# Exponentiating 5 of 16 key tiles per full unit as int16 bit patterns on VectorE, with shifts on Pool and sums and masks on TensorE

## The chip, the cores and the metric

The kernel runs on one core of a Trainium2 chip. The metric is device time in microseconds (us), the median of several executions. The kernel before takes 1201.22 us (three runs, 1200.22 to 1213.29). A difference of 2% counts. All runs below are on one core. Each experiment was timed in three rounds against the kernel before on the same chip; the experiments ran on several chips, on which the kernel before took 1202 to 1206 us (medians).

## The reference

Two attention blocks on inputs of 2048 x 512, each with 32 heads of width 16. Their outputs are laid side by side.

```python
def _A_ref(x, wqkv, wo):                       # "full": every key
    q, k, v = split(x @ wqkv)                  # 32 heads of 16
    scores = einsum("bhqd,bhkd->bhqk", q, k) * (Dh ** -0.5)
    o = einsum("bhqk,bhkd->bhqd", softmax(scores), v)
    return merge(o) @ wo
# _B_ref ("window"): the same with
    mask = (idx[:, None] - idx[None, :] >= 0) & (idx[:, None] - idx[None, :] < 256)
    scores = where(mask, scores, -1e9)
# ... setup, reshapes and the final concatenate cut
```

## The kernel before

The work comes in units of 4 heads by 512 queries: 32 full units of 16 key tiles and 32 window units. A tile is one head's 128 keys by 512 queries. Three tiles make a slot, and a slot has one tile of scores, three banks wide and with two buffers, in PSUM, the memory that TensorE's products go to. TensorE writes the scores, ScalarE exponentiates the slot in one instruction, and TensorE multiplies by the values (with a column of ones for the row sum). Projections are woven between slots in steps, and VectorE copies their results out of PSUM. A guard is a small product of this kind that gives each query an offset for its scores.

```python
def scores(self, slot):
    sps = self.ps.tile([P, SLOT, 512], FP32, name="sps", tag="sps", bufs=2)
    for b, jb in enumerate(slot["jobs"]):
        ...
        if b == 0:                       # whole-array product, overwritten by the next one
            self.nc.tensor.matmul(sps[:, 0, 0:WARM], lhsT=kT[:, gg, k0:k0 + P],
                                  rhs=qT[:, gg, 0:WARM], start=True, stop=True)
        for kt, q0, q1, o in jb.subs:
            self.nc.tensor.matmul(sps[:, b, o:o + q1 - q0], ..., tile_position=(32 * jb.j, 0))

def exps(self, slot):
    ...
    nc.scalar.activation(out=pT[:, b:e, :n], in_=sps[:, b:e, :n], func=ACT.Exp, scale=SCALE)
    # window blocks: VectorE multiplies by a triangle, or Pool selects (cut)

# run(), one slot after another:
    self.exps(sl)
    self.scores(slots[s + 2])
    self.values(...)                     # products with the values of earlier slots
    # then normalisation work that is due, then woven projection steps
```

The whole-array product has no use for the result. It keeps the array busy; b1_no_warm below shows what that does for the clock.

## Time and profile before

| engine | busy us | share of the 1204.9 us |
|---|---|---|
| ScalarE | 1094.0 | 91% |
| TensorE | 957.8 | 79% |
| VectorE | 309.1 | 26% |
| Pool | 141.4 | 12% |

The mean granted TensorE clock, as a share of full speed, was 0.958. A busy share is an average over the whole span. The pace is better read from the distance between the starts of neighbouring exponentials: 1.330 us per slot, 811 slots.

### The profile page before, as it was taken

The page shows a single profiled execution, that of the slowest core. Times are in us where ns is not written, and L with a number is a line of the kernel's source. Part 1 is how long each engine was busy: PE and PEld are TensorE (multiplying, and loading weights), DVE is VectorE, ACT ScalarE, POOL GpSimd, SP SyncE. Part 2 cuts the span into 40 slices and gives each one's busy share as a digit, 9 for nine tenths or more (in the row PEclk, how much of TensorE's full clock was granted, in tenths as well). Part 3 has the DMA queues.
Part 4 walks back from the last instruction along what each step waited for, and adds up shares of the span by engine and source line. Part 5 has one row for each costly group of instructions (what it writes and reads, how often), then busy time and mean ns, then how long its engine had stood idle before and what let it go on. Part 6 is the DMA issues. An engine that isn't in the chain of part 4 may idle for free.

```text
span 1204.9 us, 18272 instructions
## 1 busy us (share of the span) xinstructions
PE 957.8 (79%) x6762; PEld 281.9 (23%) x6859; DVE 309.1 (26%) x698; ACT 1094.0 (91%) x840; POOL 141.4 (12%) x349
## 2 busy tenths in 40 slices
PE   4888888888788888888888888868885888878754
PEld 1222222222222222222222222212221222222211
DVE  1232121133222233322233232322232222321102
ACT  2799999999899999999999999969995999999960
POOL 4000000011000011210121111111111110211100
PEclk8999999999999999899999999989997999998995
DMA  6011320111121101111111111211111111111011
GB/s 143 19 32 24 76 49 20 37 24 35 35 57 33 35 20 29 37 44 32 43 33 40 31 35 42 31 43 32 25 32 29 36 40 33 29 27 30 15 26 42
DMA packets 72921, 44.48 MB, mean 37 GB/s; under 512 B 45440, under 2 KB 64128, under 8 KB 72832
## 3 DMA queue, kind: packets, MB, share of 16 engines
q1 hardware_dynamic: 71248, 41.73, 16.0%
q10 hardware_dynamic: 1584, 1.57, 0.5%
q8 instruction: 54, 0.88, 0.3%
q14 instruction: 35, 0.29, 0.1%
HBM read 4.19 MB, written 4.19 MB: 7 GB/s over the span
## 4 chain that ended last, share of the span: by engine, by line
ACT 45%; PE 10%; issue 8%; SPq 3%; DMA 2%; DVE 2%; ACTq 0%; DVEq 0%
ACT pT L339 45%; PE sps L316 3%; PE sps L321 3%; PE ms L156 2%; PE op L371 2%; SPq L408 1%; SPq L268 1%; DMA out_dram<-ob 1%; DVE ob L300 1%; DMA oTa<-on 1%; DMA rb<-rrow 1%; DVE osb L385 1%; SPq L188 0%; DMA rrow<-den 0%; DVE pT L350 0%
## 5 line engine op out<-in xcount | busy, mean ns | idle before, releaser
L339 ACT ACTIVATE pT<-sps 128x1536 bf16<-128x1536 f32 (+4 forms) x827 | 1086.1, 1578 | 44.5 <-PE sps L321 34.3
L316 PE MATMUL sps<-qTa,kTa 128*128 128x512 bf16 x683 | 261.3, 383 | 131.1 <-ACT pT L339 125.8
L371 PE MATMUL op<-pT,va 128*32 128x512 bf16 x2048 | 275.8, 394 | 1.6 <-ACT pT L339 0.5
L321 PE MATMUL sps<-qTa,kTa 32*128 32x512 bf16 x2048 | 276.9, 389 | 0.0
L352 POOL TENSOR_SCALAR_AFFINE_SELECT pT<-pT 128x256 bf16<-128x256 bf16 (+2 forms) x224 | 105.2, 488 | 908.8 <-issue 532.4
L321 PEld LDWEIGHTS <-kTa 32*128 32x128 bf16 x2048 | 68.0, 91 | 347.5 <-issue 347.5
L371 PEld LDWEIGHTS <-va 128*32 128x32 bf16 x2048 | 69.0, 93 | 156.8 <-issue 155.8
L316 PEld LDWEIGHTS <-kTa 128*128 128x128 bf16 x683 | 65.8, 96 | 146.8 <-issue 124.4
L350 DVE TENSOR_TENSOR pT<-pT,mlo 128x128 bf16<-128x128 bf16 (+2 forms) x256 | 77.0, 345 | 85.7 <-ACT pT L339 84.7
L316 PE MATMUL sps<-qTb,kTb 128*128 128x512 bf16 x128 | 50.8, 396 | 32.7 <-ACT pT L339 30.8
L385 DVE COPY osb<-op 128x512 f32<-128x512 f32 x64 | 44.2, 691 | 87.4 <-PE op L371 87.2
L401 DVE TENSOR_TENSOR on<-osb,rb 128x512 bf16<-128x512 f32 x64 | 46.4, 726 | 77.3 <-DMA rb<-rrow 44.7
L300 DVE CAST ob<-ms 128x512 bf16<-128x512 f32 x32 | 22.1, 689 | 153.0 <-PE ms L156 153.0
L321 PE MATMUL sps<-qTb,kTb 32*128 32x384 bf16 (+2 forms) x704 | 58.0, 286 | 0.0
L371 PE MATMUL op<-pT,vb 128*32 128x384 bf16 (+2 forms) x704 | 49.6, 295 | 9.9 <-DVE osb L385 5.7
L262 DVE CAST qs<-ms 128x512 bf16<-128x512 f32 x31 | 21.3, 688 | 121.4 <-PE ms L156 121.4
L156 PE MATMUL ms<-wo,oTa 128*128 128x512 bf16 x51 | 19.9, 466 | 31.9 <-DMA oTa<-on 28.7
L392 DVE RECIPROCAL den<-den 128x16 f32<-128x16 f32 x64 | 15.1, 241 | 76.0 <-DMA den<-osb 76.0
L321 PEld LDWEIGHTS <-kTb 32*128 32x128 bf16 x704 | 17.0, 93 | 74.8 <-issue 74.8
L156 PE MATMUL ms<-xT,wq 128*128 128x512 bf16 x96 | 31.4, 384 | 3.7 <-issue 2.9
L156 PE MATMUL ms<-xT,wk 128*128 128x512 bf16 x94 | 30.3, 388 | 4.6 <-issue 1.7
L244 DVE CAST vb<-ms 128x512 bf16<-128x512 f32 x16 | 11.1, 691 | 83.1 <-PE ms L156 83.1
(47 smaller groups left out, 280.6 us busy)
## 6 DMA issues: line engine op xcount, KB each, us to landing
rb<-rrow SPq DMA_DIRECT2D x64, 256.0 KB
out_dram<-ob SPq DMA_DIRECT2D x32, 128.0 KB
kTa<-ksta SPq DMA_DIRECT2D x32, 64.0 KB
qTa<-qs SPq DMA_DIRECT2D x128, 16.0 KB
oTa<-on SPq DMA_DIRECT2D x128, 16.0 KB
kTb<-kstb SPq DMA_DIRECT2D x128, 16.0 KB
qTb<-qs SPq DMA_DIRECT2D x128, 16.0 KB
oTb<-on SPq DMA_DIRECT2D x128, 16.0 KB
```

The lines of the kernel that those rows point to most:

```text
L156: self.nc.tensor.matmul(bank, lhsT=lhs(c), rhs=rhs(c), start=(c == 0), stop=(c == NC - 1))
L262: copy(out=qs[:], in_=bank)
L300: self.nc.vector.tensor_copy(out=ob[:], in_=bank)
L316: self.nc.tensor.matmul(sps[:, 0, 0:WARM], lhsT=kT[:, gg, k0:k0 + P], rhs=qT[:, gg, 0:WARM], start=True, stop=True)
L321: self.nc.tensor.matmul(sps[:, b, o:o + q1 - q0], lhsT=kT[r, gg, k0:k0 + P], rhs=qT[r, gg, q0:q1], start=True, stop=True, tile_position=(3 ...
L339: nc.scalar.activation(out=pT[:, b:e, :n], in_=sps[:, b:e, :n], func=ACT.Exp, scale=SCALE)
L350: nc.vector.tensor_mul(out=v, in0=v, in1=self.mlo[:, 0:e - b, :])
L352: nc.gpsimd.affine_select(v, v, pattern=[[0, e - b], [-1, P]], compare_op=ALU.is_ge, fill=0.0, base=-1, channel_multiplier=1)
L371: self.nc.tensor.matmul(u["t"][32 * jb.j:32 * jb.j + 32, q0:q1], lhsT=self.v[jb.inst, kt][:, h * VP:h * VP + 32], rhs=slot["pT"][:, b, o:o ...
L385: nc.vector.tensor_copy(out=osb[:], in_=op[:])
L392: nc.vector.reciprocal(out=den[:], in_=den[:])
L401: nc.vector.tensor_mul(out=on[:], in0=osb[:], in1=st["rb"][:])
```

## The change

The intent is to take load from ScalarE, the bound. In each full unit 5 of the 16 key tiles (3 in the first unit) are exponentiated on VectorE: scale the score, round it to int16, read the bits as bf16. Two shifted copies made on Pool, weighted by two scaled copies of the values and summed on TensorE, smooth that rough exponential. A bias on ScalarE's exponentials and a lift in the scores keep both kinds on one scale. The masks of the window units move to TensorE, as products of an identity with a mask, and the whole-array product goes.

```diff
-QRING = (3, 4)
-KRING_B = 10
-VRING_B = 12
-LAGS = (6, 11, 22)
+QRING = (3, 2)
+KRING_B = 6
+VRING_B = 9
+LAGS = (7, 12, 23)
+D_KTS = (1, 4, 7, 10, 13)
 ...
     def scores(self, slot):
         sps = self.ps.tile([P, SLOT, 512], FP32, name="sps", tag="sps", bufs=2)
+                nc.tensor.matmul(sps[:, b, o:o + n * P], lhsT=self.ident[:],
+                                 rhs=self.mask[:, k:k + n, :], start=first, stop=False,
+                                 skip_group_check=True)
 ...
-            if b == 0:
-                self.nc.tensor.matmul(sps[:, 0, 0:WARM], lhsT=kT[:, gg, k0:k0 + P],
-                                      rhs=qT[:, gg, 0:WARM], start=True, stop=True)
 ...
             nc.scalar.activation(out=pT[:, b:e, :n], in_=sps[:, b:e, :n], func=ACT.Exp,
-                                 scale=SCALE)
+                                 scale=SCALE, bias=self.bias[:])
 ...
+            nc.vector.tensor_scalar(out=y[:, jb.j, :].bitcast(I16), in0=sps[:, b, :],
+                                    scalar1=0.0, scalar2=BITS, op0=ALU.max, op1=ALU.mult)
+            grp["n"] += 1
+            if grp["n"] == GH:
+                for c in SHIFTS:
+                    z = self.tile([P, GH, 512], BF16, "z", 4)
+                    nc.gpsimd.tensor_scalar(out=z[:].bitcast(I16), in0=y[:].bitcast(I16),
+                                            scalar1=c, scalar2=1.0, op0=ALU.add, op1=ALU.mult)
 ...
-            nc.vector.tensor_mul(out=on[:], in0=osb[:], in1=st["rb"][:])
+            nc.gpsimd.tensor_mul(out=on[:], in0=osb[:], in1=st["rb"][:])
 ...  (slot building, rings, plan of the woven steps cut)
```

## The prediction

> **What bounds the kernel now.** I began with the page's engine totals and slices, then the chain that ended last, then the groups kept apart by shape, then the chain and the timeline of short stretches.
>
> ```profile
> PE 957.8 (79%) x6762; PEld 281.9 (23%) x6859; DVE 309.1 (26%) x698; ACT 1094.0 (91%) x840; POOL 141.4 (12%) x349
> ACT  2799999999899999999999999969995999999960
> ACT 45%; PE 10%; issue 8%; SPq 3%; DMA 2%; DVE 2%; ACTq 0%; DVEq 0%
> ```
>
> ScalarE is full from the third slice to the last but one, and everything else has room. The chain gives it only 45% because a chain of overlapped instructions is cut in many pieces. The groups and a piece of the chain give the pace:
>
> ```profile
> L339 ACT ACTIVATE pT<-sps 128x1536 bf16<-128x1536 f32 x782 | 1055.9, 1619 | 40.9 <-PE sps L321 32.0 <-issue 5.5 <-POOL pT L352 1.4
> L339 ACT ACTIVATE pT<-sps 128x1024 bf16<-128x1024 f32 x9 | 9.9, 1105 | 1.2 <-POOL pT L352 0.8 <-issue 0.4
> ...
> 602.27 1.28 ACT pT L339
> 603.60 1.25 ACT pT L339
> 604.95 1.25 ACT pT L339
> 606.27 1.26 ACT pT L339
> 607.61 1.27 ACT pT L339
> ```
>
> One record of 1536 elements lasts 1619 ns, but neighbours start 1.33 us apart (of 775 pairs in the trace the tenth percentile and the median are 1329 and 1330 ns). Where a 1024-element exponential is followed closely, starts are 903 ns apart. So the pace is 0.833 ns per element plus about 50 ns. There are 2432 tiles of work (32 full units of 64, 32 window units of 12), three to a slot, so 811 slots: 811 x 1.330 = 1079 us. The trace has the first exponential at 34.3 us and the last end at 1164.9: 1131 us, of which some 52 are stalls. Then 40 us of tail. Sum 1205.
>
> TensorE in one slot, from the timeline:
>
> ```profile
> 700.79 0.38 PE L316 MATMUL sps<-qTa,kTa 128*128 128x512 bf16 x1 [0.32 <-ACT pT L339]
> 701.10 0.39 PE L321 MATMUL sps<-qTa,kTa 32*128 32x512 bf16 x3
> 701.42 0.40 PE L371 MATMUL op<-pT,va 128*32 128x512 bf16 x3
> 701.97 0.38 PE L156 MATMUL ms<-xT,wq 128*128 128x512 bf16 x1 [0.16 <-issue]
> 702.39 0.69 DVE L262 CAST qs<-ms 128x512 bf16<-128x512 f32 x1 [7.83 <-PE ms L156]
> ```
>
> The whole-array matmul of L316, whose result the next one overwrites, holds the array 0.31 us; three row-tiled scores 0.32; three column-tiled values some 0.32. A change of tiling costs about 0.1 us over the 0.215 us at which equal matmuls follow one another. The slot needs about 0.95 us of the 1.33, with 0.53 us more where a projection step is woven in.
>
> **What the Trainium skill says.**
> - "ScalarE: Activation LUTs", What ACT_TABLE_LOAD costs: an ACTIVATE with immediate scale and bias takes 186 ns + 0.833 ns per element, and each [128,1] pointer operand adds about 93 ns. The slope agrees (1445 ns shortest at 1536, 1018 at 1024: 0.834); the fixed part here is 165 ns, nearer to the form without a pointer. The change gives every exponential a bias tile. No run so far shows what that costs from start to start.
> - "GPSIMD Engine Reference", 4.1 Engine selection: one-input elementwise work is roughly at line rate, two-input work about twice slower than VectorE. The one-input selects here take 287, 401 and 514 ns at best for 128, 256 and 384 elements: 0.89 ns per element over 174.
> - "SBUF — State Buffer", Who interferes with whom: GpSimd and a VectorE instruction in a two-port mode, or with two SBUF inputs, exclude each other; other VectorE work does not. The new exponentials read PSUM, so they should not be touched. No run here shows it.
>
> **The change, part by part.**
> ScalarE: 31 units give up 5 x 4 tiles and the first 3 x 4: 632. Each is the third of a slot, so 632 slots have two tiles for ScalarE and the other 1800 - 1264 = 536 fill 179 slots of three. 632 x 0.903 + 179 x 1.330 = 809 us, 270 less than before. The bias pointer could add 811 x 0.093 = 75; I take two thirds, 50.
>
> VectorE: 632 tiles of 128x512 from PSUM at 0.69 us (its casts and copies of that shape are 691 ns) = 436 us. Masks (77) and the final scaling (46) leave it: 309 - 123 + 436 = 622 us. Not a bound by its sum.
>
> Pool: 158 groups of four tiles, two shifts each, 316 instructions of 2048 elements. Estimate from the selects: 174 + 2048 x 0.89 = 2.0 us, so 632 us; 64 scalings with two inputs, estimate 1.3 us each, 82; memsets 36; the selects (105) go. About 750 us. In a full unit the five groups ask for 20 us, plus 2 of other work, while the 20 slots with two tiles and 1.3 of three take ScalarE 20 to 22: Pool keeps up with little to spare, and the window slots give it rest.
>
> TensorE: L316 goes, 811 x 0.31 = 251 us. Vector groups need three value products for one: 158 x 3 sets of four column tiles at 0.215 = 102 us, in place of 632/3 x 0.32 = 67. ScalarE's values are gathered over two slots, four columns at once, so fewer changes of tiling. Masks in the scores: 640 identity products, 1024 columns per three tiles, 0.43 us and one change of tiling in each of 128 window slots = 69. The sum falls to about 750 us, under a slot's 0.9. In window slots masks, six partial scores and values come near 1.5 us against 1.33: 128 x 0.15 = 19 us lost.
>
> What I think takes much of the gain back is VectorE's **order**. Program order there is exponential of slot s, then a cast of a projection step woven into s, then the exponential of s+1. Call E the end of ScalarE's slot s. The cast's matmuls come after the scores of s+2, which wait for E: 0.05 + 0.32 + 0.1 + 0.215 + 0.416 (701.97 to 702.39 above) puts the cast at E + 1.1; 0.72 and 0.69 later the exponential of s+1 is done, at E + 2.5; only then can the scores of s+3 be written, and ScalarE starts s+3 at about E + 2.97. With two score buffers it would have started at E + 1.81. So 1.16 us are lost, more where values stand in front of the step, none where s+1 is a slot of ScalarE alone. Before, VectorE stood in no full-unit slot's path, so casts cost nothing. Casts in the stream: keys 28, values 26, queries 31, outputs 24, guards 31: 140, of which 78% (632/811) meet such a slot: 109 x 1.2 = 131 us. Copies of the accumulator wait likewise for the last values: 64 x 0.78 x 0.5 = 25. Key reductions add 28 x 0.78 x 0.69 = 15. That is 171; as such waits share their time with Pool's and with each other, I take 0.7 of it, 120.
>
> Tail: 40 us before. The staging tile of the output goes from two buffers to one, so each of eight output rows waits for the last one's transfer: about 1 us each, 48. The start stays at 34. Other stalls: the output steps now wait in the plan for their transfers, so of the 52 us I keep 10 beyond those counted.
>
> Sum: 34 + 809 + 50 + 120 + 19 + 10 + 48 = 1090 us.
>
> **The rivals.**
> 1. The gain comes almost whole: ordering hides, the bias is free. 34 + 809 + 60 + 48 = 950, with Pool's pace somewhat above it 970. For it: ring sizes and lags have been tuned with care. Against: nothing in the new order takes the casts out of VectorE's way.
> 2. Pool is the bound. Should the integer shifts take 3 us and not 2 (conversion in and out, two operations), 316 x 3 + 118 = 1066 us of Pool alone and 1150 in all. The selects, with as much to do per element, speak against it.
> 3. The order costs what I counted, and the bias its full 75: 34 + 809 + 75 + 200 + 19 + 30 + 48 = 1215, no gain.
> 4. Without the whole-array matmul TensorE's clock is granted less (0.958 on average now, 1.00 in most stretches, 0.82 to 0.86 where it idles). A clear drop would bring 1200 or more. Against: shorter slots keep the array about as busy, 750 of 1090 us.
>
> **Range and chances.** The gross gain of 270 us is sure; what is given back lies between 60 (rival 1) and 230 (rival 3), most likely near 160. I predict 1090 us, range 970 to 1190. Faster than 1177: 0.85; within 2%: 0.09; slower: 0.06 (rival 4, or rivals 2 and 3 together).
>
> **What would show it.** Starts of two-tile exponentials 0.90 us apart mean a free bias, 1.00 a paid one. Pool shifts near 2.0 us keep rival 2 away; 3 us with TensorE waiting for the shifted tiles would make it. If the order is the cause, ScalarE's busy share drops to 80% or so, its idle time ends at scores, the scores wait for VectorE rather than ScalarE, and the chain holds casts and vector exponentials by turns. A ScalarE at 90% and a time below 1000 would prove that step wrong. A granted clock under 0.9 would show rival 4. I should be wrong altogether if full-unit stretches ran slower than 1.33 us per slot.

## The result, and the profile after

The changed kernel took 1409.13 us (four runs, 1402.05 to 1418.99), against 1202.34 us for the kernel before. The ratio is 1.1705, with a 95% interval of 1.1611 to 1.1798. All ratios here are the mean time of one kernel's runs over that of the other's of the same rounds, so they are not quite the ratio of the medians quoted. Where two experiments are compared, the difference in us is that of their medians.

The page of the changed kernel: the engine totals, ScalarE's busy tenths in 40 slices, and the granted clock in tenths.

```profile
PE 1017.9 (72%) x7857; PEld 310.7 (22%) x7952; DVE 620.6 (44%) x1021; ACT 950.6 (67%) x832; POOL 719.4 (51%) x509
ACT  2446777767676776767767765668765777677770
PEclk9667877888678878879879977779887878888775
```

ScalarE was relieved of 143 us of work, but no slice is full any more: every engine now has idle time in every slice. The clock fell from 0.958 to 0.796.

The groups kept apart by shape (line, engine, operation, operands, count; then busy us and mean ns of one; then the idle time just before them and its releasers). ScalarE's two largest, VectorE's exponential, Pool's two largest:

```profile
L379 ACT ACTIVATE pT<-sps,bias 128x1024 bf16<-128x1024 f32 x608 | 666.6, 1114 | 335.4 <-PE sps L362 326.8 <-PE op L423 3.3 <-ACT pT L379 0.7
L379 ACT ACTIVATE pT<-sps,bias 128x1536 bf16<-128x1536 f32 x172 | 253.0, 1547 | 40.6 <-PE sps L362 40.1 <-ACT pT L379 0.2
L390 DVE TENSOR_SCALAR y<-sps 128x512 int16<-128x512 f32 x632 | 428.5, 686 | 364.2 <-ACT pT L379 354.7 <-issue 6.2 <-POOL on L464 2.0
L398 POOL TENSOR_SCALAR z<-y 128x2048 int16<-128x2048 int16 x316 | 599.5, 1897 | 632.5 <-DVE y L390 528.0 <-DVE den L455 37.1 <-PE sps L362 33.8
L464 POOL TENSOR_TENSOR on<-osb,rb 128x512 bf16<-128x512 f32 x64 | 80.9, 1269 | 35.3 <-DMA rb<-osb 18.6 <-DMA qTa<-gs 6.0 <-DMA oTa<-on 4.6
```

ScalarE loses its time in the two-tile slots: 327 us of waiting for scores. Pool is not the bound, for it waits 528 us for VectorE.

The view of waits (who waited for whom; total us, times, longest):

```profile
POOL z L398 <- DVE y L390: 528.0, 122, 40.2
ACT pT L379 <- PE sps L362: 388.9, 432, 4.4
DVE y L390 <- ACT pT L379: 354.7, 395, 7.9
...
PE sps L362 <- DVE y L390: 205.5, 250, 3.8
```

Read the last three lines as a ring: ScalarE waits for the scores, the scores wait for VectorE's exponential, and VectorE's exponential waits for ScalarE's. The third is the surprise. Both read the same scores, and neither needs the other's result.

A stretch of the timeline (start, duration, engine, line, operation; in brackets the idle time before and what ended it):

```profile
599.58 2.12 ACT L379 ACTIVATE pT<-sps,bias 128x1024 bf16<-128x1024 f32 x2 [0.44 <-PE sps L362]
...
600.72 0.69 DVE L390 TENSOR_SCALAR y<-sps 128x512 int16<-128x512 f32 x1 [0.86 <-ACT pT L379]
...
601.46 0.39 PE L362 MATMUL sps<-qTa,kTa 32*128 32x512 bf16 x3 [0.61 <-DVE y L390]
...
601.96 1.11 ACT L379 ACTIVATE pT<-sps,bias 128x1024 bf16<-128x1024 f32 x1 [0.27 <-PE sps L362]
...
602.75 0.69 DVE L200 CAST kst<-ms 128x512 bf16<-128x512 f32 x1 [1.19 <-PE ms L178]
603.48 0.69 DVE L201 TENSOR_REDUCE acol<-kst 128x1 f32<-128x512 bf16 x1
...
604.08 1.28 DVE L390 TENSOR_SCALAR y<-sps 128x512 int16<-128x512 f32 x2
604.82 0.39 PE L362 MATMUL sps<-qTa,kTa 32*128 32x512 bf16 x3 [2.10 <-DVE y L390]
...
605.32 1.11 ACT L379 ACTIVATE pT<-sps,bias 128x1024 bf16<-128x1024 f32 x1 [2.24 <-PE sps L362]
```

The first half shows the ring. VectorE starts at 600.72, just as the first of two exponentials ends. The scores follow 0.05 us after VectorE's end, and the next exponential 0.50 us after their start. The second half shows the order the prediction feared: a key cast and its reduction stand before the vector exponential, the scores wait 2.10 us for VectorE, and ScalarE 2.24 us for the scores.

Over the whole trace the vector exponential starts 32 or 33 ns after a ScalarE exponential ends, from the tenth percentile to the median. The ring's length follows: 1.11 (exponential) + 0.03 + 0.69 (vector) + 0.05 + 0.50 (scores) = 2.38 us for two slots, as there are two score buffers. That makes 1.19 us per slot at best, taken over two slots, where the pointer-biased exponential alone would allow 0.996. The trace has it so: where two two-tile exponentials follow each other, the start two slots on came 2.384 us later at the least and 2.387 at the lower quartile of 558. Slot by slot, of 607 starts after two-tile exponentials the quartiles were 1.141, 1.406 and 1.940 us. The prediction had counted on 0.903 to 0.996 plus a cast's wait in every sixth slot.

The semaphores in the traces say the same. In the changed kernel 619 of the 632 vector exponentials wait on the semaphore that ScalarE's instructions raise. In the kernel with a score tile of its own for VectorE (e1_own_bank, below) none does, and 407 wait on TensorE's.

Two instructions on different engines that touch one PSUM tile were put one after the other in program order here, though they read different banks of it.

### The profile page after: what moved, and what is told of

Its sections match the earlier page's. It is cut to its first block, busy times and chain, and to the rows that moved or that the text cites. A ratio compares the mean times of both kernels' runs of the same rounds, so it can differ in the third digit from the quotient of the medians.

```text
span 1417.1 us, 21178 instructions
## 1 busy us (share of the span) xinstructions
PE 1017.9 (72%) x7857; PEld 310.7 (22%) x7952; DVE 620.6 (44%) x1021; ACT 950.6 (67%) x832; POOL 719.4 (51%) x509
## 5 line engine op out<-in xcount | busy, mean ns | idle before, releaser
L379 ACT ACTIVATE pT<-sps,bias 128x1024 bf16<-128x1024 f32 (+3 forms) x819 | 942.7, 1187 | 398.3 <-PE sps L362 388.9
L398 POOL TENSOR_SCALAR z<-y 128x2048 int16<-128x2048 int16 x316 | 599.5, 1897 | 632.5 <-DVE y L390 528.0
L390 DVE TENSOR_SCALAR y<-sps 128x512 int16<-128x512 f32 x632 | 428.5, 686 | 364.2 <-ACT pT L379 354.7
L362 PE MATMUL sps<-qTa,kTa 32*128 32x512 bf16 x2048 | 367.5, 462 | 239.0 <-DVE y L390 205.5
L351 PE MATMUL sps<-mask,ident 128*128 128x128 bf16 (+1 forms) x640 | 95.1, 271 | 86.9 <-DVE y L390 71.6
L423 PE MATMUL op<-y,va 128*32 128x512 bf16 x632 | 116.4, 500 | 0.0
L423 PE MATMUL op<-z,v1x 128*32 128x512 bf16 x632 | 110.1, 467 | 0.0
L423 PE MATMUL op<-z,v0x 128*32 128x512 bf16 x632 | 106.9, 475 | 0.0
L464 POOL TENSOR_TENSOR on<-osb,rb 128x512 bf16<-128x512 f32 x64 | 80.9, 1269 | 35.3 <-DMA rb<-osb 18.6
L351 PEld LDWEIGHTS <-ident 128*128 128x128 bf16 x640 | 56.5, 103 | 147.6 <-issue 136.2
```

What stands on the lines that cost most here:

```text
L351: nc.tensor.matmul(sps[:, b, o:o + n * P], lhsT=self.ident[:], rhs=self.mask[:, k:k + n, :], start=first, stop=False, skip_group_check=True)
L362: nc.tensor.matmul(sps[:, b, o:o + q1 - q0], lhsT=kT[r, gg, k0:k0 + P], rhs=qT[r, gg, q0:q1], start=not jb.blocks, stop=True, tile_positio ...
L390: nc.vector.tensor_scalar(out=y[:, jb.j, :].bitcast(I16), in0=sps[:, b, :], scalar1=0.0, scalar2=BITS, op0=ALU.max, op1=ALU.mult)
L398: nc.gpsimd.tensor_scalar(out=z[:].bitcast(I16), in0=y[:].bitcast(I16), scalar1=c, scalar2=1.0, op0=ALU.add, op1=ALU.mult)
L423: self.nc.tensor.matmul(u["t"][32 * j:32 * j + 32, q0:q1], lhsT=v[:, h * VP:h * VP + 32], rhs=src, start=(j not in u["started"]), stop=Fal ...
L464: nc.gpsimd.tensor_mul(out=on[:], in0=osb[:], in1=st["rb"][:])
```

## The experiments

The first theory after reading the trace was the ring ("serial"). The rivals were the copies' order, the bias tile and the clock.

**1. The vector tile's scores in a PSUM tile of their own (e1_own_bank).** The same banks in number: two tiles of two banks and two of one.

```diff
-        sps = self.ps.tile([P, SLOT, 512], FP32, name="sps", tag="sps", bufs=2)
+        sa = self.ps.tile([P, 2, 512], FP32, name="sa", tag="sa", bufs=2)   # ScalarE's
+        sv = self.ps.tile([P, 512], FP32, name="sv", tag="sv", bufs=2)      # third tile
```

> Scores of the vector tile go to a PSUM tile of their own, so the vector exponential of a slot no longer waits for ScalarE's exponential of the same slot. Serial theory (one score tile shared by two readers puts VectorE behind ScalarE in every slot and is the largest part of the 1409 us): time falls to 1130 to 1220 us, the vector exponential starts before ScalarE's of its slot has ended, ScalarE's busy share goes above 78%. Clock theory (TensorE's lower clock, 0.80, is the cause and not a consequence): time stays above 1350 and the clock near 0.80. Order theory alone (casts woven in front of the vector exponentials): above 1300.

1308.16 us (1304.51 to 1309.01), ratio 1.085, clock 0.828. That is 101 us less than the changed kernel: right in direction, short of the 1130 to 1220 expected. ScalarE's busy share rose to 73%, not above 78%, and the time fell into the band set for the order alone (above 1300), so the ring was not the largest part. Waits of this kernel:

```profile
DVE y L396 <- PE sv L367: 170.5, 221, 7.9
ACT pT L385 <- PE sv L367: 156.0, 138, 5.2
...
PE sv L367 <- DVE y L396: 126.1, 100, 4.0
```

VectorE no longer waits for ScalarE: 499 of its 632 exponentials ran mostly beside one of ScalarE's, 319 before. The ring explains about 100 us, and what was left had to be something else. Scores still waited 126 us for VectorE.

**2. The whole-array product put back (e2_warm).**

```diff
+            nc.tensor.matmul(sps[:, 0, :], lhsT=kT_whole, rhs=qT_whole, start=True, stop=True)
             # then the scores of a full slot, which overwrite it
```

> The changed kernel with the whole-array product of the kernel before put back in front of the scores of full-unit slots. Clock theory: the granted clock rises above 0.92 and the time falls by 100 us or more, to under 1310. Serial theory: the clock may rise, but the product lies on the path from the vector exponential's end to the next scores, 0.31 us in some 680 slots, so the time does not fall: 1400 to 1600.

1487.27 us (1482.22 to 1492.29), ratio 1.2346. The clock rose from 0.796 to 0.867, and the kernel became 78 us slower: the product stands in the ring.

**3. No tile on VectorE (e3_no_vec).** `D_KTS = ()`, all else as in the changed kernel.

> The changed kernel with no key tile given to VectorE: only masks by identity products, no whole-array product, bias tile, new plan and rings remain. Serial theory: 34 + 811 x 1.423 (pace with a bias tile as the changed kernel's trace shows it) + 48 + 20 to 60 of stalls = 1255 to 1300 us, faster than the changed kernel although ScalarE does all of the work. Clock theory: clock under 0.88 without the whole-array product and over 1320 us.

1270.26 us (1268.28 to 1273.03), ratio 1.0546, clock 0.703. The page of this kernel:

```profile
PE 999.8 (79%) x6601; PEld 295.2 (23%) x6688; DVE 198.8 (16%) x379; ACT 1168.6 (92%) x840; POOL 117.9 (9%) x193
PEclk9975565556677877667788887768786678576555
```

ScalarE is full again, at an even lower clock. Its 1536-element exponentials start 1.423 us apart, against 1.330 before. The difference of 93 ns is the bias tile: 783 such slots x 0.093 = 73 us, which covers all of the 65 us that this kernel is slower than the kernel before. So with ScalarE as the bound the pointer is paid in full, and the low clock costs next to nothing: ScalarE was busy for 97% of the time at half speed and for 97% of it at full speed. The new rings, lags, plan and masks, which this kernel keeps, cost nothing that shows here either.

**4. The kernel before without its whole-array product (b1_no_warm).**

> The kernel before without its whole-array product and nothing else. Does the product hold the clock? If it does: clock under 0.90 (0.958 before), and time longer only as far as TensorE then exceeds ScalarE's 1.33 us per slot: 1200 to 1260. If not: clock 0.93 to 1.0 and 1190 to 1210 us.

1232.47 us (1229.25 to 1233.05), ratio 1.0225. The clock fell from 0.958 to 0.639. So the product does hold the clock, and with its own cost taken off that is worth about 2% there (1.0204 to 1.0247).

**5. The copies moved behind the vector exponentials (e4_order, e7_order_only).** The copy of a woven step is issued up to two slots later than its matmuls, after that slot's vector exponential, and no new step starts before it. e4_order adds this to e1_own_bank, e7_order_only to the changed kernel with the shared tile.

```diff
+    def hold(self, f):
+        self.copy = (self.slot + 2, f)
 ...
-            self.v_evac(i, t, bank, self.nc.vector.tensor_copy)
+            self.hold(lambda: self.v_evac(i, t, bank, self.nc.vector.tensor_copy))
 ...  (keys, queries, guards and output rows alike)
             self.exps(s, sl)
+            if self.copy is not None and self.copy[0] <= s:
+                self.flush()
```

> e1_own_bank (1308 us) with the copies of the woven projection steps and guards issued on VectorE one to two slots later, behind the next vector exponentials. Order theory of the prediction (109 events of about 1.2 us and some more): 1308 - 120 = about 1190, 1160 to 1230. If the remaining stalls come from TensorE's clock (0.83) or from values and scores on TensorE: 1280 to 1310.

1185.97 us (1185.21 to 1189.83), ratio 0.9845, clock 0.883: 122 us less than e1_own_bank.

> The changed kernel, score tile still shared, with only the copies issued later behind the vector exponentials. If the order costs its own share, as between e1 and e4 (122 us): 1409 - 80 to 130 = 1280 to 1330. If the shared tile hides it, because the vector exponential is late in every slot anyway: above 1370.

1292.42 us (1288.24 to 1293.52), ratio 1.0713, clock 0.859: 117 us less than the changed kernel. In e4_order scores wait a third as long for VectorE as in e1_own_bank:

```profile
PE sv L388 <- DVE y L417: 46.3, 29, 4.8
```

The two factors add up. The order is worth 117 and 122 us with and without the shared tile, the tile of its own 101 and 106 us with the old order and the new.

**6. The bias as an immediate (e5_imm on e1_own_bank, e6_order_imm on e4_order, e15_imm_only on the changed kernel).**

```diff
-                                 scale=SCALE, bias=self.bias[:])
+                                 scale=SCALE, bias=BIAS)
```

> e1_own_bank with the bias as a number in the instruction instead of a [128,1] tile. If the bias tile costs 93 ns at each of 990 exponentials and ScalarE's pace counts in most slots: 1308 - 50 to 90 = 1220 to 1260, starts of two-tile exponentials 903 ns apart at best instead of 996. If ScalarE mostly waits for scores anyway: 1290 to 1308.

1259.47 us (1251.94 to 1267.52), ratio 1.0444: 49 us less than e1_own_bank.

> e4 and e5 together. If both stalls are independent: 1308 - 120 - 75 = about 1115, 1080 to 1170, faster than the kernel before. If TensorE at its granted clock is then the bound: above 1180.

1158.9 us (1153.23 to 1161.56), ratio 0.9603: 27 us less than e4_order. With the three repairs together the idea beats the kernel before by 4%.

> The changed kernel with nothing but the bias as a number instead of a tile. With the score tile still shared, each slot runs ScalarE's exponential and then VectorE's, so the 93 ns lie on that loop: 1409 - 40 to 75 = 1335 to 1370. If ScalarE's length does not count there: above 1395.

1384.21 us (1382.87 to 1385.54), ratio 1.1489: 25 us less, under the 40 to 75 expected. The trace shows how: the shortest start-to-start of two tiles fell from 996 to 903 ns, but on the ring the 93 ns count once in two slots (lower quartile 2.387 us before, 2.297 now), and where ScalarE waits for something else they are hidden.

**7. The clock, from the other side (e8_all_warm, e12_fill_after, e13_fill_e6, e14_fill_all_e6).** e8_all_warm is e6_order_imm with the whole-array product. The other three add whole-array products of zeros into the open accumulator at the end of a slot: in some 470 slots without a projection step of the changed kernel, in the odd ones of those of e6_order_imm (some 230), in all of them.

```diff
+            if self.op is not None and len(self.op["started"]) == GH and s != self.last:
+                self.nc.tensor.matmul(self.op["t"][:], lhsT=self.zero[:], rhs=self.v[0, 0][:, 0:512],
+                                      start=False, stop=False, skip_group_check=True)
```

> e6 with the whole-array product put back in front of the scores of full-unit slots. Clock theory: clock from about 0.8 to above 0.9 and at least 30 us faster than e6. Against it: 683 products of 0.31 us fill TensorE's slot (0.8 + 0.3 us against ScalarE's 0.9), so 50 us or more slower than e6.

1206.27 us (1203.21 to 1210.5), ratio 1.0005: clock up from 0.889 to 0.93, 47 us slower, close to the 50 or more expected if TensorE's slot is full.

> The changed kernel with a whole-array product of zeros added to the open accumulator at the end of each slot that has no projection step (some 470), where TensorE would next wait for VectorE; unlike e2 it does not stand between the vector exponential and the next scores. If TensorE's low clock (0.80) is a cause of the 1409 us: clock above 0.88 and 1340 to 1385. If it is only a consequence of the waits: clock may rise, time 1395 to 1430.

1434.41 us (1430.83 to 1438.21), ratio 1.1899: clock up from 0.796 to 0.845, 25 us slower, a little beyond the band for a mere consequence.

> e6 (1159 us, clock 0.889) with the same product of zeros in odd slots without a projection step (some 230), where TensorE has the least to do. Clock a cause of what is left: clock above 0.92, 1115 to 1145. Only a consequence: 1150 to 1180.

1170.35 us (1164.14 to 1175.8), ratio 0.9712, clock 0.905, 11 us slower, in the band for a mere consequence.

> As e13 in all slots without a projection step (some 470). Clock a cause: clock above 0.94, within 20 us of e13 either way. TensorE's time the bound: 20 to 60 us slower than e13.

1194.46 us (1189.92 to 1199.55), ratio 0.9915, clock 0.918, 36 us slower than e6_order_imm and 24 slower than e13_fill_e6: in the band for TensorE's time as the bound. Five times a raised clock went with a longer time. These runs do not show that the clock is free, since each bought it with work that costs time too.

The traces tell the order of events. The clock in them is 1.0 or 0.5 and changes at steps of 3.41 us. In the changed kernel TensorE was idle for 53% (median) of the 3.41 us before each of the 65 falls, against 24% in the other steps at full speed; in e6_order_imm it was 57% before 31 falls, against 6%. So TensorE's idle time comes first, and the low clock is a consequence of the waits. Whether it then lengthens them is less clear. In the 3.41 us before and after a fall ScalarE was idle for 38% and 60% of the time in e6_order_imm, but for 42% and 36% in the changed kernel. Of ScalarE's idle time in the changed kernel, 128 us passed while TensorE had no wait over 0.3 us, and 92 of them lie in the 40% of the time at half speed.

**8. What is left in the repaired kernel.** With order and bias repaired, the prediction's own sum would say 1090 - 120 - 50 = 920 us. The split of three-tile slots into two instructions adds 9 (172 x 0.051). The measured 1159 is 230 above that.

*Less work for TensorE (e10_no_z).* e6_order_imm without the value products of the shifted tiles. Its output is wrong, which doesn't matter for the time.

```diff
-                for t, src in enumerate(terms):
+                for t, src in enumerate(terms[:1]):
```

> e6 without the value products of the shifted tiles (Pool still makes them, nothing reads them; the result is wrong on purpose). 115 us of e6's stalls lie where TensorE was busy. If TensorE's load in a slot is the bound there: 1159 - 60 to 110 = 1050 to 1100. If clock or transfers decide: above 1140.

1156.59 us (1152.88 to 1163.58), ratio 0.9612: no gain, the band for clock or transfers. Here is e10_no_z's page:

```profile
PE 938.8 (82%) x6601; PEld 274.8 (24%) x6688; DVE 630.4 (55%) x1021; ACT 862.9 (75%) x1008; POOL 720.8 (63%) x509
PEclk9679797798888879888878877979987889786775
```

And that of e6_order_imm:

```profile
PE 947.2 (82%) x7857; PEld 279.6 (24%) x7952; DVE 633.0 (55%) x1021; ACT 861.2 (75%) x1008; POOL 721.0 (63%) x509
PEclk9789998898988899889898978989987899889985
```

A sixth of the matmuls went (7857 to 6601), yet TensorE's busy time and the kernel's time stayed: the clock fell from 0.889 to 0.827 and each product took longer. TensorE's sum is not the bound, but its clock gave back part of the relief, so this run does not clear TensorE altogether.

*Buffers and lags (e9_lags).* Longer lags of the normalisation, two buffers for query copies and output rows, paid for by two window value tiles.

```diff
-VRING_B = 9
-LAGS = (7, 12, 23)
+VRING_B = 7
+LAGS = (11, 16, 24)
-        qs = self.tile([P, 512], BF16, "qs", 1)        # and "ob" likewise
+        qs = self.tile([P, 512], BF16, "qs", 2)
```

> e6 with two buffers again for the query and output copies and the reciprocal issued four slots later (paid for with a shorter ring of values). In e6 VectorE stood 6 to 8 us at a time before a query copy or a reciprocal that waited for a transfer: 67 us of ScalarE's stalls. If cutting those rings and lags costs that: 1159 - 30 to 65 = 1095 to 1130. If something else takes the place: above 1145.

1146.61 us (1142.41 to 1151.6), ratio 0.9512: 12 us less, in the band for "something else takes the place".

*TensorE's load spread (e11_odd).* On top, projection steps only in slots without value products of vector groups, unless the plan is pressed.

```diff
-            while credit >= 1.0 and self.fill(s, tasks, done):
+            while credit >= (1.0 if s % 2 or s < 60 else 1.7) and self.fill(s, tasks, done):
```

> e9 with projection steps woven only into the slots that have no value products of their own, as long as the plan allows it. If the unevenness of TensorE's slots (0.3 + 0.75 + 0.54 us in one, 0.3 in the next) makes its stalls: 20 to 60 us faster than e9. If not: within 1% of it.

1136.06 us (1133.53 to 1143.96), ratio 0.9434: 11 us less, which is within the 1% set for "if not", and the two kernels' runs overlap. So a gain is not shown.

*Four tiles for five (e16_four), and none in the first unit (e17_first).*

```diff
-D_KTS = (1, 4, 7, 10, 13)
+D_KTS = (1, 5, 9, 13)                     # e16_four
-(vec if kt in (D_KTS if units else D_KTS[:3]) else act).append(job)
+(vec if units and kt in D_KTS else act).append(job)      # e17_first
```

> The best version so far (e11_odd, 1136 us) with four instead of five key tiles of each full unit on VectorE: 124 tiles go back to ScalarE, whose floor by the sum of starts rises from 809 to 508 x 0.903 + 303 x 1.330 = 862 us, 53 more. If five tiles are too many, because TensorE, VectorE and Pool set the pace in most slots, the time stays within 1120 to 1150 all the same. If ScalarE sets the pace, it rises by the whole of that, to 1180 to 1195. The TensorE clock should stay within 0.03 of 0.879 either way.

1137.98 us (1136.83 to 1147.52), ratio 0.9455: no change. The pages' totals of e16_four and then of e11_odd:

```profile
PE 937.7 (83%) x7608; PEld 288.2 (25%) x7704; DVE 551.3 (49%) x895; ACT 915.4 (81%) x1136; POOL 603.7 (53%) x447
```

```profile
PE 929.1 (81%) x7854; PEld 279.2 (24%) x7952; DVE 636.7 (56%) x1021; ACT 861.1 (75%) x1008; POOL 721.7 (63%) x509
```

ScalarE took on 54 us more, VectorE 85 and Pool 118 us less, and nothing moved. The fifth tile is worth nothing here. ScalarE's sum alone is not the bound, for then 53 us would have been added. One run cannot tell whether no engine's sum counts, or whether what ScalarE lost was given back by VectorE and Pool.

> The best version so far (e11_odd, 1136 us) with no key tile of the very first unit on VectorE, since the first unit was slow in the traces (ScalarE worked 34.7 of the 66 us from 34 to 100 us) and VectorE has copies of projections there. If VectorE's load is what slows the first unit: 5 to 20 us less, 1115 to 1131. If it is TensorE's projections and the transfers: no change to 3 us more, 1133 to 1142.

1133.59 us (1130.35 to 1136.02), ratio 0.9393, interval 0.9345 to 0.944. The gain of 2.5 us over e11_odd lies inside the spread of their runs. This is the best version: 6% faster than the kernel before.

## Why the prediction was wrong

**ScalarE's relief: right as a sum, wrong as a pace.** The step that failed is "Each is the third of a slot, so 632 slots have two tiles for ScalarE ... 632 x 0.903 + 179 x 1.330 = 809 us". It takes for granted that ScalarE and VectorE read one slot's scores side by side. In the program VectorE's read was placed behind ScalarE's, since both touch one tile. From the ring above, 632 x (1.19 - 0.996) = 123 us would follow; undoing it gave 101 and 106. No step of the prediction asked which engine a new reader of an old tile waits for. The Trainium skill, "PSUM — Partial Sum Buffer", Specifications (TRN2), says that the two engines can use PSUM in parallel at full bandwidth as long as no bank collides. The trace agrees: in e11_odd the 548 vector exponentials that ran mostly beside one of ScalarE's took 686 ns on average, the 84 others 673. The hardware allowed the overlap, and the program did not.

**Order: right in mechanism; in size too, with some luck.** Predicted 120, measured 117 and 122. But the 120 was a sum of 171 times a factor of 0.7 that no trace gave, and 25 of the 171 were copies of the accumulator, which the experiments left in place. The timeline has the cast, the reduction, the waiting scores and the idle ScalarE just as the prediction drew them. The place where it can be undone is VectorE's program order.

**Bias: the mechanism right, the size from 25 to 49.** Predicted 50, measured 49 and 27 with a tile of its own, 25 on the ring. From start to start it is the 93 ns that the skill's page gives, where ScalarE does not wait.

**Pool: right.** Estimated 2.0 and 1.3 us an instruction, measured 1.897 and 1.269; 750 us in all, measured 719. Rival 2 is out.

**VectorE: right as a sum, with one thing overlooked.** 622 us predicted, 620.6 measured; the exponential 0.69 us. But short copies from SBUF to SBUF grew: the absolute value of the queries (the mq group) took 314 ns before, 347 without tiles on VectorE, 523 in the changed kernel and 921 in e11_odd, where Pool is busiest. The prediction quoted the page that says why (VectorE in a two-port mode and GpSimd exclude each other) and applied it to the exponentials alone. The trace of e11_odd agrees: the 8 of these 32 instructions with no Pool instruction beside them took 294 ns, and each of the 20 that took over 500 ns ended some 0.29 us after a Pool instruction did. Some 38 us of VectorE time went there in e11_odd (mq and nega 52.9 us against 14.8 before).

**The clock (rival 4): it did fall, first of all as a consequence; what it cost is open.** The argument against it, that shorter slots keep the array about as busy, failed. TensorE's sum was put at about 750 us, where the terms given come to 811 (957.8 - 251 + 35 + 69), and it measured 1017.9, lengthened by the low clock itself. And the array waited: in the changed kernel 40% of the time between the first and last exponential ran at half speed (score products 602 instead of 384 ns), 5% before. Experiments 2 and 7 and the clock's own record make it a consequence of the waits; experiment 3 and b1_no_warm show that it costs about 2% or less where ScalarE sets the pace. A rough upper estimate for the changed kernel: exponentials started 1.50 us apart in its full-speed stretches and 1.89 in the others, so 283 x 0.39 = 110 us, in which the stalls that brought the clock down are counted too.

**"I keep 10" for other stalls: the other large miss.** The overrun of 319 us is about 105 for the shared tile and about 215 of stalls that the sum did not have. After all repairs some 200 remain (1133.6 against 929). In e6_order_imm's trace ScalarE was idle for some 224 us between exponentials. Put down to TensorE's longest wait in each gap, about 105 passed while TensorE had no wait over 0.3 us, 73 in 22 waits for VectorE to free a score tile, and the rest behind copies and transfers. No single load was found behind them: fewer value products (but no less busy a TensorE), and less Pool and VectorE work with more for ScalarE, left the time where it was. More TensorE work made it longer. The half-speed stretches hold 120 of the 224 us in 20% of the time, and whether the low clock lengthens stalls that something else began stays open. The mask products in the window slots (predicted 19 us) were not tested alone; in the changed kernel's trace ScalarE waited 2 us in all for scores of window slots.

**Start and tail: right.** First exponential at 34.9 us (34), tail 41 us (48).

## What to carry to other kernels

When a second engine is given part of a buffer, ask what its read waits for: two readers of one PSUM tile ran one after the other here, and a tile of its own for the second reader gave back about 100 us at no cost in banks. An engine that enters the loop of the critical engine brings its whole program order with it, so long copies there must be moved behind the loop's own work (some 120 us here). Count the ring of waits per buffer before summing loads: with no engine more than 72% busy, none was the bound by its sum.

## What the Trainium skill lacked or had wrong

- "ScalarE: Activation LUTs", What ACT_TABLE_LOAD costs: its 93 ns per pointer operand holds exactly (1423 against 1330 ns from start to start). But it gives an overlap of about 93 ns between back-to-back exponentials, which would put starts of 1536 elements 1373 ns apart without a pointer (an estimate from its figures, 186 + 0.833 x 1536 - 93); the runs show 1330.
- "TensorE: Matmul & The Clock Gate", Part 1: its two clock states agree with the traces (1.0 and 0.5 alone, score products of 384 and 602 ns). It speaks of idle and busy windows and gives no figure for how idle a window must be. Here the clock fell after steps of 3.41 us in which TensorE was idle for about half of the time (medians of 49% in the kernel before, 53% in the changed kernel, 41% in b1_no_warm), and it came back only after steps with at most 13% idle.
